# A ConvNeXt block in two phases: every third block stored whole, 96-row reloads, and all loads of phase 2 on the SyncE queue

## The chip, the core and the metric

The kernel runs on one core of a Trainium2 chip. That core has five engines with a queue of instructions each: TensorE (PE, matrix products; its weight loads are listed as PEld), VectorE (DVE), ScalarE (ACT), GpSimd (POOL) and SyncE (SP, which here only issues transfers). Data moves between the chip's memory (HBM) and the on-chip buffers through 16 DMA engines. A transfer can be issued from the queue of SP (the profile's q1, "hardware_dynamic") or from that of GpSimd (q0, "software_dynamic"); both use the same 16 engines. The metric is the device time of one execution, in microseconds (us). The kernel before takes 1479.7 us, the median of three runs from 1476.99 to 1480.79.

## The reference, cut to what matters

```python
# x: (1, 512, 512, 96) bf16; dw: (3, 3, 96); w1: (96, 384); w2: (384, 96)
out = depthwise_conv3x3(x, dw)                     # zero padding
h = layernorm(out, axis=-1)                        # over the 96 channels, no scale
h = gelu(einsum('bhwc,ce->bhwe', h, w1))
gx = sqrt((h * h).sum(axis=(1, 2)) + 1e-6)         # over the whole image, per channel
nx = gx / (gx.mean(axis=-1) + 1e-6)
h = grn_gamma * (h * nx) + grn_beta + h
return x + einsum('bhwe,ec->bhwc', h, w2)
```

The sum `gx` runs over the whole image. So nothing can be multiplied with `w2` before every pixel has gone through the gelu once, and the hidden tensor `h` (512 x 512 x 384 in bf16, some 201 MB) is far too big to be kept on chip.

## The kernel before, in words

The image is cut into 128 blocks of four rows (2048 pixels). `yn` is a block after the convolution and the layernorm, 96 channels by 2048 pixels; `g` is the same block after `w1` and gelu, 128 x 6144 values (1536 KB).

**Phase 1** (to about 980 us) makes `yn` and `g` of every block and gathers the sums of squares. Its order is written out by hand: one block enters per slot, and in a slot stand the convolution, the normalisation, the matrix product with `w1`, the gelu and the squares of different blocks. `yn` of every block is written to HBM (`stage_write`) and read back as a 96-row tile `ynT` (`stage_read`, from SP), since the product wants channels on the partitions. The squares are made in two ways: a block's `g` has four quarters, and `cm_quads(q)` says how many of them VectorE handles (`BATCH_NORM_STATS2`); the others go to TensorE (`gram_next`). Blocks for which `is_whole(q)` holds have their `g` written to HBM, in three pieces of 512 KB, one in each following slot (`store_next`); there are 35 of these, `q % 10` being 0, 3 or 7 below block 114. Five blocks (`HELD`) keep `g` on chip, three (`KEPT`) keep `ynT`. Phase 1 ends with the sums and the scaled weights `W2s`.

**Phase 2** (from about 980 us) goes through the 128 blocks in the order `ORDER`, which spreads the 40 blocks that have their `g` among the 88 that must make it again. A position n needs:

- its `g`: kept on chip, or loaded from `g_dram` into one of two buffers `gl` (1536 KB; called G here), or made again from `ynT` (Y here). Y has a ring of six buffers, and making `g` again takes four units of three matmuls of 512 columns and one gelu of 128 x 1536 each (`cm_unit`), run about two blocks ahead of use (`LEAD`, `pace`), with three buffers `gr`.
- its `x`: loaded into one of five buffers `xr` (384 KB; X here). GpSimd adds the bias to it and writes `xb` (`stage_xb`), two positions ahead.
- the product: `stage_mm2` runs four parts of 12 matmuls with `W2s`; after each part VectorE adds `xb` and writes a quarter of `o_sb` (four buffers).
- the store of `o_sb` to the output (384 KB; O here), issued from SP one position later (`stage_out`).

G and X for position n + 5 (`PRE`) are issued in position n. In phase 2 of the kernel before, SP issues Y and O, GpSimd issues G and X between its additions. The first eight positions (`FIRST`) keep the written order; behind them the scheduler of the language orders each queue, and it puts a Y some ten positions ahead of its use, where it waits for its buffer in the ring.

`yn_rows(q)` reads Y as 128 rows of 4 KB, the 96 rows of block q and 32 of the next one. The weights `w1p` have zeros in rows 96 to 127, so the extra rows add nothing. `yn_src(q)` reads the 96 rows alone; phase 1 uses it.

In the profile most instructions carry line 35, that of the helper `InOrder` which records them, so groups are told apart by their tiles. Lines of their own are 279 (X), 290 (G), 294 (Y), 324 (`xb`) and 352 (O).

Of the kernel before, what the change touches and what calls it, by code (L numbers as in the profile page):

```python
# [12 lines left out]
GR = 4  # L13
# [3 lines left out]
FILL = (6, 15)  # L17
BATCH = 4
NHELD = 5
WHOLE = (0, 3, 7)  # L20
NTAIL = 14
GRB = 3

# [33 lines left out]
def kernel(  # L57
# [16 lines left out]
    B, H, W, C = x.shape  # L74
# [6 lines left out]
    NBLK = H // GR  # L81
# [5 lines left out]
    yn_dram = dram.tile([NBLK, C, GR * W], bf16, name="yn_dram")  # L87
    r_dram = dram.tile([NBLK, GR, W], bf16, name="r_dram")

    TAIL0 = NBLK - NTAIL  # L90
# [3 lines left out]
    def is_held(q):  # L94
        return q in HELD

    def is_whole(q):
        return q < TAIL0 and q % 10 in WHOLE

    def cm_quads(q):  # L100
        if is_whole(q) or is_held(q):
            return NQ
        if q > HELD[0]:
            return 1
        return 2 if q >= NBLK - 16 or (q - 1) % 10 in WHOLE else 3

    whole = [q for q in range(NBLK) if is_whole(q)]
    g_dram = dram.tile([len(whole), 128, NQ * NCH * QW], bf16, name="g_dram")

# [11 lines left out]

    def yn_src(q):
        return yn_dram[q].rearrange("c (r w) -> c r w", r=GR)

    def yn_rows(q):
        return yn_dram[q:q + 2].rearrange("q c (r w) -> (q c) r w", r=GR)[0:128]

    def yn_dst(q, r):
        return yn_dram[q].rearrange("(c i) (r w) -> r c i w", i=NI, r=GR)[r]
# [17 lines left out]
    B2bc_f = consts.tile([128, C], f32, name="B2bc_f")  # L147

    NENT = sum(cm_quads(q) for q in range(NBLK - 2))
    NLAST = cm_quads(NBLK - 2) + cm_quads(NBLK - 1)  # L150
    GROUPS = [min(32, NENT - k) for k in range(0, NENT, 32)] + [NLAST]
    NACC = len(GROUPS)
# [9 lines left out]
    W2s = consts.tile([128, NCH, C], bf16, name="W2s")  # L162
    B2c = consts.tile([128, C], f32, name="B2c")
    free = [[q for q in range(NBLK) if is_whole(q)], list(HELD)]
    free = [v for i, q in enumerate(free[0]) for v in (free[1][i:i + 1] + [q])]
    made_q = KEPT + [q for q in range(NBLK) if not is_whole(q) and not is_held(q) and q not in KEPT]
# [17 lines left out]
    with ExitStack() as p1:  # L184
# [57 lines left out]
        for b in range(min(2, NBLK)):  # L242
# [3 lines left out]
                       in_=zrow[:, None, :NI * GR * 32].to_broadcast([128, 3, NI * GR * 32]), func=ACTF.Identity)  # L246
# [28 lines left out]
        def load_xr(n, pq):  # L275
            q = ORDER[n]
            r0 = q * GR
            xr = late.xr.tile([128, PXP, C], bf16, name="xr")
            pq.dma_start(out=xr[:], in_=x[0, r0:r0 + GR].rearrange("r w c -> (r w) c").rearrange(  # L279
                "(p g) c -> p g c", g=PXP))  # L280
            grp.setdefault(q, {})["xr"] = xr

        def load_rest(n, sq, pq):
            q = ORDER[n]
            v = grp.setdefault(q, {})
            if is_held(q):
                v["g"] = gs[q]
            elif is_whole(q):
                v["g"] = late.gl.tile([128, NQ, NCH, QW], bf16, name="gl")
                pq.dma_start(out=v["g"][:].rearrange("p t j w -> p (t j w)"), in_=g_dram[whole.index(q)])  # L290
            else:
                ynt = yn_ring[SLOTS[nth_made[q] % NYT]]
                if q not in KEPT:
                    sq.dma_start(out=ynt[:], in_=yn_rows(q))
                v["ynt"] = ynt

        def recompute(q, t):
# [22 lines left out]
        def stage_xb(q, pq, bias):  # L320
            if q is None:
                return
            xb = late.xb.tile([128, PXP, C], f32, name="xb")
            pq.tensor_tensor(out=xb[:], in0=grp[q]["xr"][:],  # L324
                                    in1=bias[:, None, :].to_broadcast([128, PXP, C]), op=ALU.add)
            grp[q]["xb"] = xb

        def stage_mm2(n, q):
            g, xb = grp[q]["g"], grp[q]["xb"]
            GQ = QW // 128  # L330
            o_sb = late.o.tile([128, PXP, C], bf16, name="o_sb")
            for sub in range(NSUB):
                O = out_bank()
                for gl_ in range(GPS):
                    gg = sub * GPS + gl_
                    for j in range(NCH):
                        t, c = gg // GQ, gg % GQ * 128
                        pe.matmul(O[:, gl_, :], lhsT=g[:, t, j, c:c + 128], rhs=W2s[:, j, :],
                                   start=(j == 0), stop=(j == NCH - 1))
                dve.tensor_tensor(out=o_sb[:, sub * GPS:(sub + 1) * GPS, :], in0=O,  # L340
                                   in1=xb[:, sub * GPS:(sub + 1) * GPS, :], op=ALU.add)
                if n == NBLK - 1:
                    out_part(q, o_sb, sub)
                if sub == NSUB - 1 and q in nth_made:
                    used[0] += 1
                pace(n, sub)
            grp.pop(q)
            return o_sb

        def stage_out(q, o_sb):  # L350
            r0 = q * GR
            nc.sync.dma_start(
                out=out[0, r0:r0 + GR].rearrange("r w c -> (r w) c").rearrange("(p g) c -> p g c", g=PXP),
                in_=o_sb[:])

        PRE = 5
# [42 lines left out]
        n = 0  # L399
# [255 lines left out]
        for q in range(NBLK):  # L655
            if q == NBLK - 2:
                e_ = 32 * (NACC - 1)
            ents[q] = e_
            e_ += cm_quads(q)
# [166 lines left out]
        for s in range(last_slot + 1):  # L826
# [120 lines left out]
            if s == last_slot:  # L947
                for n in range(PRE):
                    load_rest(n, sp, sp)
# [19 lines left out]
        r = gi[:].bitcast(f32)  # L969
        for it in range(3):  # L970
# [5 lines left out]
            r = rn_[:]  # L976
# [21 lines left out]
    with p2:  # L998
        def out_part(q, o_sb, sub):
            r0 = q * GR  # L1000
            nc.sync.dma_start(
                out=out[0, r0:r0 + GR].rearrange("r w c -> (r w) c").rearrange(
                    "(p g) c -> p g c", g=PXP)[:, sub * GPS:(sub + 1) * GPS],
                in_=o_sb[:, sub * GPS:(sub + 1) * GPS])

        held = None
        FIRST = 8
        for n, q in enumerate(ORDER):
            sq, pq = (sp, pool) if n < FIRST else (nc.sync, nc.gpsimd)
            if n + PRE < NBLK:  # L1010
                load_rest(n + PRE, sq, pq)
                load_xr(n + PRE, pq)
            if 3 <= n + 2 < NBLK:
                stage_xb(ORDER[n + 2], pq, B2c)
            if n == NBLK - 1:
                stage_out(*held)
                held = None
            o_sb = stage_mm2(n, q)
            if held:
                stage_out(*held)  # L1020
            held = (q, o_sb)
# [30 lines left out]
```

## Time and profile before

| What | us or share |
|---|---|
| times of the three runs | 1480.79, 1479.70, 1476.99 |
| profiled execution: span from first to last instruction | 1480.8 |
| PE, ACT, POOL, DVE busy, share of the span | 94%, 96%, 88%, 80% |
| POOL and ACT busy in phase 2, 1100 to 1450 us | 338.1 and 335.7 of 350 |
| DMA engines busy, 300 to 850 us and 1100 to 1450 us | 0.83 and 1.02 |
| bytes moved per second in the same stretches | 261 and 410 GB/s |
| granted TensorE clock, mean | 0.994 |

The profiled execution's span equals the longest of the three times within rounding. A busy share says how long an engine had an instruction in hand in a stretch. "Idle before" of a group of instructions is how long its engine waited in front of them, and the name behind the arrow is what ended the wait. The DMA share is the mean over the 16 engines of the time that packets took; packets that overlap on an engine can bring it a little above 1. The three resources TensorE, ScalarE and GpSimd are all busy for 96 to 97% of the stretch from 1100 to 1450 us, and the DMA engines for all of it.

### The profile page before, as it was taken

Reading aid. Unit: us, or ns where it says so; the run is one execution under the profiler, and the core shown is the slowest. Engines: PE = TensorE matmul, PEld = TensorE weight load, DVE = VectorE, ACT = ScalarE, POOL = GpSimd, SP = SyncE. Lnnn points to the kernel's source line nnn. Section 1 sums busy time; section 2 is a strip of 40 time slices with the busy share of each in tenths; the row PEclk is TensorE's granted clock in tenths of the full one; section 3 lists DMA queues with packets and bytes.
Section 4 is the critical chain, followed back from the end, with each engine's and each line's share of the span. In section 5 each row is a group of like instructions: output and inputs, shape, how many; then the busy total and the mean of one; then the engine's idle time right before and its main releaser. Section 6 shows DMA issues by size and latency. Waiting matters only on the chain.

```text
span 1480.8 us, 54225 instructions
## 1 busy us (share of the span) xinstructions
PE 1391.3 (94%) x23125; PEld 810.4 (55%) x23125; DVE 1182.0 (80%) x2135; ACT 1414.4 (96%) x1595; POOL 1300.3 (88%) x922
## 2 busy tenths in 40 slices
PE   8888999999999999999999997789999999999998
PEld 3434444444444444444444445467777777776776
DVE  7849989999999999999999987965555555555555
ACT  7888989999999999999999999999999999999997
POOL 3459889998998999998999987569999999999997
PEclk9999999999999999999999999999999999999999
DMA  5568788788888888888888866669999999999997
GB/s 180 179 205 255 241 253 280 228 271 260 260 248 264 258 264 255 276 253 254 263 258 266 263 216 195 195 225 409 366 359 402 417 416 413 419 410 417 411 412 282
DMA packets 167768, 433.08 MB, mean 292 GB/s; under 512 B 31558, under 2 KB 81318, under 8 KB 163046
## 3 DMA queue, kind: packets, MB, share of 16 engines
q1 hardware_dynamic: 151284, 326.04, 66.3%
q0 software_dynamic: 14880, 103.43, 17.6%
q8 instruction: 181, 2.97, 0.8%
q14 instruction: 61, 0.50, 0.1%
q10 hardware_dynamic: 1362, 0.15, 0.1%
HBM read 273.30 MB, written 156.22 MB: 290 GB/s over the span
## 4 chain that ended last, share of the span: by engine, by line
PE 30%; ACT 24%; DMA 19%; POOL 13%; DVE 6%; issue 4%; SPq 4%; POOLq 0%; ACTq 0%; DVEq 0%
PE PS L35 30%; ACT g L35 16%; DMA out_dram<-o_sb 9%; POOL yn L35 6%; ACT y_bf L35 5%; POOL ysq L35 5%; SPq L35 4%; DMA yn_dram<-yn 3%; DVE bst L35 3%; DMA xin<-in_x_dram 2%; DMA rbc<-r_dram 2%; DMA ynT<-yn_dram 1%; DMA g_dram<-g 1%; DVE o_sb L35 1%; ACT xT L35 1%
## 5 line engine op out<-in xcount | busy, mean ns | idle before, releaser
L35 ACT ACTIVATE g<-PS 128x512 bf16<-128x512 f32 (+2 forms) x1062 | 727.7, 864 | 16.5 <-PE PS L35 15.6
L35 DVE BATCH_NORM_STATS2 bst<-g 128x6 f32<-128x512 bf16 x1110 | 671.3, 672 | 35.4 <-ACT g L35 34.5
L35 PE MATMUL PS<-ynT,w1p 128*128 128x512 bf16 x2181 | 609.6, 381 | 23.6 <-ACT g L35 5.4
L35 ACT ACTIVATE gr<-PS 128x1536 bf16<-128x1536 f32 x360 | 498.5, 1459 | 18.8 <-PE PS L35 13.8
L35 POOL TENSOR_TENSOR yn<-y_bf,rbc 128x1536 bf16<-128x1536 bf16 x126 | 391.3, 3108 | 77.3 <-ACT rbc L35 21.9
L35 DVE TENSOR_TENSOR o_sb<-PS,xb 128x384 bf16<-128x384 f32 x512 | 277.3, 556 | 227.0 <-PE PS L35 190.1
L324 POOL TENSOR_TENSOR xb<-xr,B2c 128x1536 f32<-128x1536 bf16 x118 | 368.1, 3133 | 4.3 <-DVE o_sb L35 2.0
L35 PE MATMUL PS<-xT,Wq 64*32 64x511 bf16 (+1 forms) x9198 | 340.5, 389 | 26.2 <-ACT y_bf L35 8.1
L35 POOL TENSOR_TENSOR ysq<-y_bf 128x1536 bf16<-128x1536 bf16 x114 | 313.6, 2752 | 12.8 <-ACT y_bf L35 12.8
L35 PEld LDWEIGHTS <-w1p 128*128 128x128 bf16 x2181 | 171.6, 98 | 222.0 <-issue 133.4
L35 PEld LDWEIGHTS <-gr 128*128 128x128 bf16 x4296 | 212.1, 98 | 68.9 <-issue 12.0
L35 PE MATMUL PS<-W2s,gr 128*128 128x96 bf16 x4224 | 223.5, 206 | 8.2 <-DVE o_sb L35 8.0
L35 PEld LDWEIGHTS <-Wq 64*32 64x32 bf16 x9216 | 111.9, 90 | 193.3 <-issue 145.9
L35 ACT ACTIVATE y_bf<-PS 128x1536 bf16<-128x1536 f32 (+2 forms) x135 | 199.4, 1482 | 17.4 <-PE PS L35 13.3
L35 DVE STREAM_TRANSPOSE xT<-xin 128x576 f32<-128x576 f32 (+1 forms) x256 | 181.4, 748 | 8.1 <-DMA xin<-in_x_dram 8.1
L35 PEld LDWEIGHTS <-g 128*128 128x128 bf16 x1704 | 104.9, 98 | 86.3 <-issue 54.3
L35 PE MATMUL PS<-w1p,ynT 128*128 128x256 bf16 (+2 forms) x822 | 125.8, 273 | 8.0 <-ACT xT L35 3.2
L35 PE MATMUL PS<-g 128*128 128x128 bf16 x1464 | 122.6, 220 | 2.9 <-DVE PS L35 2.6
L35 PEld LDWEIGHTS <-gl 128*128 128x128 bf16 x1680 | 82.8, 98 | 26.8 <-issue 5.0
L35 PE MATMUL PS<-W2s,gl 128*128 128x96 bf16 x1680 | 89.5, 206 | 3.4 <-DVE o_sb L35 3.2
L35 PEld LDWEIGHTS <-ynT 128*128 128x128 bf16 x822 | 64.1, 97 | 31.5 <-issue 13.7
L279 POOL DMA_DIRECT2D xr<-in_x_dram x115 | 63.7, 555 | 14.2 <-POOL xb L324 14.2
(105 smaller groups left out, 576.5 us busy)
## 6 DMA issues: line engine op xcount, KB each, us to landing
xin<-in_x_dram SPq DMA_DIRECT2D x126, 432.0 KB
g_dram<-g SPq DMA_DIRECT2D x105, 512.0 KB
gl<-g_dram POOLq DMA_DIRECT2D x35, 1536.0 KB, 11.3
yn_dram<-yn SPq DMA_DIRECT2D x512, 96.0 KB
ynT<-yn_dram SPq DMA_DIRECT2D x128, 384.0 KB
out_dram<-o_sb SPq DMA_DIRECT2D x127, 384.0 KB
xr<-in_x_dram POOLq DMA_DIRECT2D x123, 384.0 KB, 6.9
ynT<-yn_dram SPq DMA_DIRECT2D x85, 512.0 KB
```

The source lines that it names most:

```text
L35: r = f(*a, **k)
L279: pq.dma_start(out=xr[:], in_=x[0, r0:r0 + GR].rearrange("r w c -> (r w) c").rearrange("(p g) c -> p g c", g=PXP))
L324: pq.tensor_tensor(out=xb[:], in0=grp[q]["xr"][:], in1=bias[:, None, :].to_broadcast([128, PXP, C]), op=ALU.add)
```

## The change

Three things change together. Every third block below 114 is stored whole: 38 blocks, so that 85 are made again instead of 88, and `cm_quads` follows the new pattern. Phase 2 reads Y as the 96 rows of its block (384 KB instead of 512 KB). G and X of phase 2 are issued from SP, like Y and O; GpSimd issues no transfer there.

```diff
-WHOLE = (0, 3, 7)
...
     def is_whole(q):
-        return q < TAIL0 and q % 10 in WHOLE
+        return q < TAIL0 and q % 3 == 0
...
-        return 2 if q >= NBLK - 16 or (q - 1) % 10 in WHOLE else 3
+        return 2 if q >= NBLK - 16 or q % 3 == 1 else 3
...
-    def yn_rows(q):
-        return yn_dram[q:q + 2].rearrange("q c (r w) -> (q c) r w", r=GR)[0:128]
...
-                    sq.dma_start(out=ynt[:], in_=yn_rows(q))
+                    sq.dma_start(out=ynt[:C], in_=yn_src(q))
...
             if n + PRE < NBLK:
-                load_rest(n + PRE, sq, pq)
-                load_xr(n + PRE, pq)
+                load_rest(n + PRE, sq, sq)
+                load_xr(n + PRE, sq)
```

In the built program of the changed kernel, SP's queue in phase 2 holds, position after position, the load for n + 5 (Y or G, where there is one), X for n + 5, and O for n - 1.

## The prediction

> **What bounds the kernel now.** I read the page's slices first, to see the stages, then the busy table by stage.
>
> ```profile
> DMA  5568788788888888888888866669999999999997
> GB/s 180 179 205 255 241 253 280 228 271 260 260 248 264 258 264 255 276 253 254 263 258 266 263 216 195 195 225 409 366 359 402 417 416 413 419 410 417 411 412 282
> ```
> ```profile
> core 0: us, PE busy (x) PEld busy (x) DVE busy (x) ACT busy (x) POOL busy (x), PEclk, DMA share, GB/s
> 300.00:850.00 550.00, 527.12 (x9544) 259.14 (x9543) 544.63 (x933) 546.12 (x777) 515.84 (x384) 1.00 0.83 261
> ...
> 980.00:1100.00 120.00, 118.46 (x1739) 88.12 (x1738) 66.96 (x124) 117.25 (x86) 113.99 (x67) 1.00 0.98 370
> 1100.00:1450.00 350.00, 340.60 (x4962) 251.78 (x4959) 190.88 (x353) 335.74 (x243) 338.14 (x205) 1.00 1.02 410
> ```
>
> Phase 1 is held by ACT and DVE (99% busy), and DMA has room (0.83). Phase 2 runs at a flat 410 GB/s with every DMA engine busy. VectorE makes four `o_sb` quarters per block, so 353 in 350 us are 88.25 blocks: 3.966 us a block. Next, the groups and the waits of that stretch:
>
> ```profile
> L35 ACT ACTIVATE gr<-PS 128x1536 bf16<-128x1536 f32 x243 | 336.5, 1451 | 14.3 <-PE PS L35 10.7 <-ACT gr L35 0.3
> ...
> L324 POOL TENSOR_TENSOR xb<-xr,B2c 128x1536 f32<-128x1536 bf16 x89 | 277.6, 3134 | 1.6 <-DVE o_sb L35 0.6
> ...
> L279 POOL DMA_DIRECT2D xr<-in_x_dram x88 | 48.8, 555 | 10.1 <-POOL xb L324 10.1
> ```
> ```profile
> DVE o_sb L35 <- DMA out_dram<-o_sb: 30.8, 21, 2.7
> ```
>
> The 30.8 us say who is slowest: VectorE finds all four `o_sb` still on their way out, and TensorE then waits 9.3 us for VectorE. The chain of waits has stores of 12.6 to 14.0 us from issue to landing at just these places. So DMA sets the pace, with the engines close behind. Per block ACT needs 336.5/243 = 1.385 us for each of 2.75 units, 3.81 us. GpSimd needs 3.13 + 0.555 + 0.32 x 0.536 = 3.86 us. TensorE: in the timeline 12 matmuls of `stage_mm2` alone take 0.51 us (1213.09 to 1213.60), with one unit behind them 1.15 us (1213.60 to 1214.75), so a unit is 0.64 and a block 4 x 0.51 + 2.75 x 0.64 = 3.80 us.
>
> **The change, part by part.** Last, the transfers of 1100 to 1450 us (queues: packets, MB, share of the 16 engines' time; issues: count, size, median us from issue to landing):
>
> ```profile
> q0 software_dynamic: 10952, 77.23, 54.1%
> q1 hardware_dynamic: 21194, 65.66, 46.9%
> ...
> gl<-g_dram POOLq DMA_DIRECT2D x28, 1536.0 KB, 11.4
> out_dram<-o_sb SPq DMA_DIRECT2D x89, 384.0 KB
> xr<-in_x_dram POOLq DMA_DIRECT2D x88, 384.0 KB, 7.0
> ynT<-yn_dram SPq DMA_DIRECT2D x59, 512.0 KB
> ```
>
> *Bytes.* Before, 16 positions hold 5 G, 11 Y, 16 X, 16 O: 5 x 1536 + 11 x 512 + 32 x 384 = 25600 KB, 1600 KB a block. After, 3 positions hold 1 G, 2 Y, 3 X, 3 O: 1536 + 2 x 384 + 6 x 384 = 4608 KB, 1536 KB a block. That is 4.0% less: more G, cheaper Y. At the same rate a block takes 3.966 x 0.96 = 3.81 us.
>
> *Is a 96-row Y really 25% cheaper?* Its price lies between 384 and 512 parts of the old one. The nearest row is a 96-row read of phase 1 that was almost alone, from 28.1 to 28.5 us:
>
> ```profile
> DMA packets 37, 0.14 MB, mean 348 GB/s; under 512 B 3, under 2 KB 3, under 8 KB 37
> ...
> q1 hardware_dynamic: 37, 0.14, 84.9%
> ```
>
> 348/0.849 = 410 GB/s per full share, the rate of phase 2 with 128 rows (410/1.02 = 402). So I price it by bytes. The other end, 512 as before, gives 1536 + 1024 + 2304 = 4864 KB, 1621 KB a block, 4.02 us.
>
> [...]
>
> *One queue.* X and G move from q0 to q1. By the rows above q0 moves 77.23 MB in 0.541 x 350 us of 16 engines, 25.5 GB/s each, and q1 25.0. So the moved 54% may cost 2% more: 1.1% of 3.81, 0.04 us; the other end is nothing, since G keeps its long rows. I take 0.03: 3.84 us. Whether a single queue holds the rate is read where q0 was nearly empty, 1112.3 to 1113.7 us:
>
> ```profile
> q1 hardware_dynamic: 187, 0.60, 105.9%
> q0 software_dynamic: 1, 0.00, 0.0%
> ```
>
> It does: 430 GB/s over that stretch, stores and reads mixed. The far end is phase 1, where SP's queue alone made 261/0.83 = 314 GB/s, with many packets under 2 KB: 1573 kB/314 = 5.0 us.
>
> *SP's own time.* An issue takes 0.33 us there (0.43 for an X; a G by the nearest row, a 512 KB store of phase 1, 0.37 to 0.72): three a block, at most 1.5 of 3.84 us. G waits for TensorE to leave the block one before the current one (two `gl` buffers, six positions apart); X and O stand behind it, but O waits for VectorE's end of the same block anyway, some 0.6 us later. Cost nothing; without that cover, at the list's last G (positions 125 and 127 lie close), one O comes a block late. Y is issued 5 positions ahead instead of ten; it is wanted about 2.3 positions ahead, and SP reaches it almost a block early, so 3.3 x 3.84 = 12.7 us are left against the landings of 7 to 14 us. That is tight, like the store's own slack of three blocks; late loads are the dangerous rival.
>
> *Engines.* GpSimd loses its issues: 3.13 us a block. ACT makes 2.67 units: 3.69 us. TensorE: 3.75 us by the sum above; from 1040 to 1100 us, at 364 GB/s, it did 16 blocks in 60 us, 3.75 each, with 2.75 units. So once the stores stop holding VectorE, TensorE is next, 0.1 us below the DMA. This caps the gain.
>
> *Phase 1.* Nine more store pieces of 512 KB. One piece goes per slot and three fall due per three slots, so none queue up; DMA share goes from 0.83 to about 0.86. VectorE's quarters stay 370 against 369. Bounds: 0, and 9 x 1.27 us (512 KB at 410 GB/s) = 11 us if each were exposed; ACT at 99% covers them, I take 1 us. The same for the end of the list: 1 us.
>
> *Sum.* From 1100 us on there are 353 + 32 quarters, 96 blocks: 96 x (3.966 - 3.84) = 12.1 us. From 980 to 1100, 31 blocks at 3.87, mostly held by TensorE: 2 us. Less the 2 us of phase 1 and the end: 12 us. 1480.8 - 12 = 1468.8 in the profiled execution; the median of the runs lies 1.1 us lower, so 1468.
>
> **The rivals.**
>
> *The 96 rows cost as much as 128.* For: only the short isolated read speaks against it. Then 96 x 0.054 = 5 us lost in the steady part, nothing won before it, 2 lost: 1487. Chance 0.17.
>
> *One queue in order makes loads late* (the other side: slower). Place: Y behind O on SP, and every transfer behind a G of 1.57 MB, 3.8 us at 410 GB/s. For: store landings are already 14 us at saturation, and Y's lead is halved. Against: what comes late lowers the demand, and a full queue keeps the rate; a stall costs only when the engines run dry. It decides from 0.126 us a block, 0.4 us in three blocks; one microsecond per three blocks is 96/3 - 12 = 20 us over, 1501; at phase 1's rate of 314 GB/s it would be 96 x 1.04 = 100 us over. Chance 0.15.
>
> *The gain is half.* TensorE, ACT and DMA lie within 4% and disturb each other, or phase 1 pays for the nine pieces: 3.90 us a block or 6 us in phase 1, 1474. Chance 0.14.
>
> That the change does not do what it says I exclude: the built queues hold 38 G, 82 Y of 96 rows, and no transfer on GpSimd in phase 2.
>
> **How the numbers follow.** The main case has 0.54. A measurement of this kernel can tell about 0.3%, 4.4 us, from no change. The main case and half of the "half" case lie beyond that: faster 0.54 + 0.07 = 0.61. The other half of it and the lower edge of the first rival: same 0.07 + 0.02 = 0.09. The rest of the first rival and the second: slower 0.15 + 0.15 = 0.30. The main case alone spans 1462 (pace 3.78, near TensorE's floor) to 1473. The range goes from 1460 to 1494, which takes in the first rival and the beginning of the second.
>
> **What would show it.** In the middle of phase 2: 3.84 us a block (about 91 blocks in 350 us), still some 405 to 410 GB/s at a DMA share near 1, all in q1; waits of `o_sb` for stores below 30.8 us; GpSimd near 82% busy; gelu of `gr` at 2.67 a block; phase 2 beginning near 980 us. Wrong if TensorE or ACT wait for `ynT` or `gl` (late loads), if the rate per DMA share falls with 96-row reads in flight (first rival), or if phase 2 begins later than 983 us.

## The result and the profile after

The changed kernel takes 1540.05 us (median of four runs), the kernel before 1478.35 us beside it: a ratio of 1.0402, 95% interval 1.0363 to 1.0441. It is 4% slower where 0.8% faster was forecast, and it lies outside the range. One of the four executions of e1_rows96 below took 1904 us at a granted clock of 0.654 and is left out of its ratio.

The page's slices of the changed kernel, DMA busy share and bytes moved, show that phase 1 is as before and phase 2 is not:

```profile
DMA  5668788887888888888888756699999999999997
GB/s 174 196 201 251 248 268 269 269 280 252 267 266 255 262 283 269 278 269 277 264 268 260 238 158 204 232 353 351 357 343 341 350 324 341 341 347 330 338 336 275
```

Phase 2 starts at the same time (the first `o_sb` is written at 973.1 us, before at 975.5) and lasts longer (to 1535.4, before 1477.4). The busy table of 1100 to 1450 us:

```profile
core 0: us, PE busy (x) PEld busy (x) DVE busy (x) ACT busy (x) POOL busy (x), PEclk, DMA share, GB/s
...
1100.00:1450.00 350.00, 297.82 (x4209) 219.75 (x4207) 161.84 (x301) 280.53 (x201) 233.87 (x76) 0.97 1.02 340
```

VectorE wrote 301 quarters instead of 353, so a block takes 350/75.25 = 4.65 us, before 3.97. All engines are less busy than before; only the DMA share is unchanged at 1.02, and with it the engines moved 340 GB/s instead of 410. The transfers of that stretch:

```profile
q1 hardware_dynamic: 30939, 118.44, 101.1%
...
gl<-g_dram SPq DMA_DIRECT2D x25, 1536.0 KB
xr<-in_x_dram SPq DMA_DIRECT2D x75, 384.0 KB
out_dram<-o_sb SPq DMA_DIRECT2D x74, 384.0 KB
ynT<-yn_dram SPq DMA_DIRECT2D x50, 384.0 KB
```

118.44 MB in 1.011 x 350 us of 16 engines is 20.9 GB/s each; before, the two queues made 25.0 and 25.5. The bytes per block did fall to 1573 kB, and 1573 kB at 340 GB/s are 4.63 us: the whole loss is the rate. The waits of the same stretch have the face of late loads and stores (line numbers are one to four lower in the changed kernel: the helper's is 34, X 275, G 286, Y 290, `xb` 320, O 348):

```profile
DVE o_sb L34 <- DMA out_dram<-o_sb: 84.4, 35, 4.9
POOL xb L320 <- DMA xr<-in_x_dram: 75.8, 28, 4.9
ACT gr L34 <- PE PS L34: 66.7, 45, 5.2
```

But late transfers alone don't show a bad order of issues here, where the 16 DMA engines have no idle time (share 1.02). A lower rate looks the same from the engines, and e3 below, with the same order and queue, decides between the two. The chain of waits from 1200 to 1300 us passes from transfer to transfer, nearly without an engine in it:

```profile
1189.66 12.52 DMA xr<-in_x_dram
...
1202.19 12.76 DMA ynT<-yn_dram
...
1215.01 13.16 DMA out_dram<-o_sb
```

### The profile page after: what moved, and what is told of

It reads as the page before. It is cut to its first block, busy times and chain, and to the rows that moved or that the text cites. A ratio compares the mean times of both kernels' runs of the same rounds, so it can differ in the third digit from the quotient of the medians.

```text
span 1538.6 us, 54241 instructions
## 1 busy us (share of the span) xinstructions
PE 1395.2 (91%) x23104; PEld 815.9 (53%) x23104; DVE 1180.2 (77%) x2132; ACT 1402.6 (91%) x1583; POOL 1215.5 (79%) x764
## 4 chain that ended last, share of the span: by engine, by line
DMA 37%; ACT 24%; PE 15%; POOL 11%; SPq 5%; issue 4%; DVE 3%; POOLq 0%; ACTq 0%; DVEq 0%
ACT g L34 17%; PE PS L34 15%; DMA out_dram<-o_sb 12%; DMA ynT<-yn_dram 9%; DMA xr<-in_x_dram 6%; POOL yn L34 6%; ACT y_bf L34 5%; SPq L34 5%; POOL ysq L34 4%; DMA yn_dram<-yn 3%; DMA gl<-g_dram 2%; DMA rbc<-r_dram 2%; DMA xin<-in_x_dram 2%; DVE bst L34 1%; ACT xT L34 1%
## 5 line engine op out<-in xcount | busy, mean ns | idle before, releaser
L34 ACT ACTIVATE gr<-PS 128x1536 bf16<-128x1536 f32 x348 | 486.6, 1455 | 89.0 <-PE PS L34 84.0
L34 PEld LDWEIGHTS <-w1p 128*128 128x128 bf16 x2142 | 168.5, 98 | 222.1 <-issue 125.9
L34 PEld LDWEIGHTS <-gl 128*128 128x128 bf16 x1824 | 89.2, 98 | 26.7 <-issue 3.7
L34 PE MATMUL PS<-W2s,gl 128*128 128x96 bf16 x1824 | 95.8, 206 | 2.7 <-DVE o_sb L34 2.6
L34 PE MATMUL PS<-rowsel,ysq 128*128 128x4 bf16 x1536 | 56.6, 166 | 11.9 <-POOL ysq L34 11.2
```

The lines of the kernel that those rows point to most:

```text
L34: r = f(*a, **k)
```

## The experiments

Three edits came together, so most runs take one, two or the whole of them. Two theories stood against each other: the **rows theory** (a load of 96 rows slows the packets on the DMA engines, its own and its neighbours') and the **queue theory** (a single queue, served in order, loses the rate or makes loads late). Every ratio below is to the kernel before on the same chip, with its 95% interval; us a block is 350 us over a quarter of the `o_sb` writes from 1100 to 1450 us. e7, e8 and e11 were executed twice each, the others four to twelve times. Three kernels serve for their times alone: e4 leaves out one of a block's four image rows, e8 32 of its 96 channels, and e7 puts every second Y beside the wrong weights.

| Run | Y | G, X from | whole | ratio | us a block | GB/s |
|---|---|---|---|---|---|---|
| before | 128 rows | GpSimd | 35 | 1 | 3.97 | 410 |
| after | 96 | SP | 38 | 1.0402 (1.0363 to 1.0441) | 4.65 | 340 |
| e1_rows96 | 96 | GpSimd | 35 | 1.0139 (1.0105 to 1.0173) | 4.22 | 369 |
| e2_spq | 128 | SP | 35 | 0.9974 (0.9944 to 1.0005) | 3.95 | 411 |
| e3_after_128rows | 128 | SP | 38 | 1.0035 (1.0007 to 1.0063) | 4.02 | 411 |
| e4_after_128x3k | 128 x 3 KB | SP | 38 | 0.9934 (0.9909 to 0.9960) | 3.85 | 405 |
| e5_after_gpsimd | 96 | GpSimd | 38 | 1.0188 (1.0128 to 1.0247) | 4.23 | 374 |
| e6_whole38 | 128 | GpSimd | 38 | 1.0018 (0.9988 to 1.0048) | 4.03 | 412 |
| e7_after_alternate | 96, in turn low and high | SP | 38 | 1.0373 (1.0292 to 1.0454) | 4.50 | 353 |
| e8_after_64rows | 64 | SP | 38 | 1.0272 (1.0175 to 1.0368) | 4.39 | 337 |
| e9_spq_rows96 | 96 | SP | 35 | 1.0386 (1.0339 to 1.0433) | 4.53 | 339 |
| e10_after_y_gpsimd | 96, from GpSimd | SP | 38 | 1.0266 (1.0225 to 1.0308) | 4.38 | 357 |
| e11_after_112rows | 112 | SP | 38 | 1.0557 (1.0498 to 1.0616) | 4.79 | 339 |
| e12_spq_33whole | 128 | SP | 33 | 1.0015 (0.9990 to 1.0040) | 3.98 | 400 |

### One edit alone

The 96 rows alone, on the kernel before:

```diff
-                    sq.dma_start(out=ynt[:], in_=yn_rows(q))
+                    sq.dma_start(out=ynt[:C], in_=yn_src(q))
```

> The kernel before with one edit: phase 2 reads Y as 96 rows; 35 whole blocks, G and X still from GpSimd. Rows theory (a 96-row load slows the DMA engines' packets, its own and those beside it): most of the 60 us of the whole change is here, 1515 to 1545 us, with 340 to 370 GB/s at a DMA share near 1 in the middle of phase 2 and packets' time per byte up. Queue theory (it is the single queue in order that loses the rate): 96 rows save 1408 of 25600 KB per 16 blocks, DMA falls behind the engines, 3.80 us a block instead of 3.97, 1462 to 1470 us.

It is 1.39% slower, about 21 us, though a block of phase 2 moves 5.5% fewer bytes. The queue theory, which wanted a gain here, falls; the rows theory has the sign right but had expected most of the 60 us. The transfers of e1 from 1100 to 1450 us:

```profile
q0 software_dynamic: 10439, 73.87, 57.5%
q1 hardware_dynamic: 18163, 54.54, 42.5%
```

q0 holds G and X, which this edit doesn't touch. It made 77.23 MB at 54.1% before (25.5 GB/s on each engine) and 73.87 MB at 57.5% here: 22.9. So a 96-row load makes the loads beside it dearer, not only itself.

The queue alone, on the kernel before:

```diff
-                load_rest(n + PRE, sq, pq)
-                load_xr(n + PRE, pq)
+                load_rest(n + PRE, sq, sq)
+                load_xr(n + PRE, sq)
```

> The kernel before with one edit: all loads of phase 2 from SP; 35 whole blocks, Y of 128 rows. Rows theory: within 10 us of the kernel before (1470 to 1490), DMA still near 405 GB/s. Queue theory: 1515 to 1545 us, rate near 340 GB/s, waits for ynT, gl and xr on PE, DVE and POOL.

No difference that can be told: 0.9974, the interval just reaches 1. The busy row of 1100 to 1450 us and its one queue:

```profile
1100.00:1450.00 350.00, 342.66 (x4996) 253.66 (x4994) 192.29 (x354) 338.04 (x246) 277.86 (x89) 1.00 1.02 411
```
```profile
q1 hardware_dynamic: 37589, 143.24, 101.5%
```

One queue moves 411 GB/s, what two moved; GpSimd falls from 338.1 to 277.9 us busy, and nothing follows, since it was not the one in front. The queue's own waits of this run hold a warning for readers:

```profile
SPq L352 <- DMA gl<-g_dram: 79.7, 24, 4.1
SPq L279 <- DMA out_dram<-o_sb: 45.5, 76, 1.3
```

A store on SP here ends its wait when a G lands, which it doesn't need. In this program a transfer on SP uses the completion semaphore of the transfer eight before it on the queue, so at most eight are under way: 226 of the 264 issues of this stretch begin within 0.15 us of that landing, and none before it. In the changed kernel the same two waits stand first and third in SP's list, with 114.5 and 39.7 us. They look like the culprit there, and in e2 they cost nothing.

The whole blocks alone, on the kernel before:

```diff
-        return q < TAIL0 and q % 10 in WHOLE
+        return q < TAIL0 and q % 3 == 0
...
-        return 2 if q >= NBLK - 16 or (q - 1) % 10 in WHOLE else 3
+        return 2 if q >= NBLK - 16 or q % 3 == 1 else 3
```

> The kernel before with one edit: 38 whole blocks instead of 35. Y of 128 rows, G and X from GpSimd. 1621 KB a block instead of 1600: 96 blocks x 0.05 us = 5 us slower, 1483 to 1492 us, at 410 GB/s. If the three extra blocks weighed more in phase 1 (nine more store pieces), phase 2 begins more than 3 us later than before.

1.0018, within the interval no difference in the total; in the middle of phase 2 a block takes 4.03 us, as the 1621 KB say (4.02). The first `o_sb` came at 978.6 us, 3.1 later than before; but among these runs it lies between 971.2 and 985.8 in no order by the number of whole blocks, so nothing is read from it.

### Is it the bytes or the rows?

The changed kernel, Y read as 128 rows again (this run and the next define `yn_rows` as in the kernel before):

```diff
...
-                    sq.dma_start(out=ynt[:C], in_=yn_src(q))
+                    sq.dma_start(out=ynt[:], in_=yn_rows(q))
```

> The changed kernel with Y read as 128 rows again (38 whole blocks, all loads from SP). 1621 KB a block instead of 1600. Rows theory: 4.02 us a block, 1480 to 1492 us, no stretched packets. Queue theory: as slow as the changed kernel or slower, 1535 to 1560 us.

1.0035: with more bytes, the 4% are gone. Then the same 384 KB as the changed kernel, in 128 rows of 3 KB:

```diff
...
-                    sq.dma_start(out=ynt[:C], in_=yn_src(q))
+                    sq.dma_start(out=ynt[:, 0:3], in_=yn_rows(q)[:, 0:3])
```

> The changed kernel with Y read as 128 rows of 3 KB, the same 384 KB as its 96 rows of 4 KB (the last image row of each block is left out of the load, so the made-again blocks are computed with old data there; the work is the same). Same bytes, same queue, other layout. Rows theory: the pace that the bytes allow, 3.81 to 3.85 us a block, 1465 to 1475 us. Queue theory, and any theory of bytes: no better than the changed kernel, 1530 to 1545 us.

It is faster than the kernel before by 0.66%, at 3.85 us a block; the 1476.0 us are 1 us over the range of the rows theory. VectorE's busy time with its number of instructions (the `o_sb` quarters), the clock, the DMA share and GB/s from 1100 to 1450 us, first of the changed kernel, then of e3, then of e4:

```profile
1100.00:1450.00 350.00, 161.84 (x301) 0.97 1.02 340
```
```profile
1100.00:1450.00 350.00, 187.33 (x348) 1.00 1.02 411
```
```profile
1100.00:1450.00 350.00, 196.17 (x364) 1.00 1.02 405
```

All three have the same queue, the same order and the same share of DMA time. e4 has the bytes of the changed kernel, in rows of 3 KB that lie apart in HBM. e3 has more bytes, in rows of 4 KB without gaps, like those of the changed kernel. Both keep the rate, so neither the bytes nor the length of a row is the reason. What is left, and shown as the cause, is the number of rows, which is the number of partitions that a load writes. By the two ratios 69 us lie between the changed kernel and e4 (0.0468 of 1480).

The single packets in the traces agree (1100 to 1450 us; in these runs only Y has packets of 4 KB there, X and O have 3 KB). In e3 the median packet of 3 KB takes 121 ns, and 0.4% take over one and a half times as long. In the changed kernel the median is 125 ns, but 20% are over that mark, and a tenth take 221 ns or more. A 3 KB packet that begins there with no Y packet under way takes 131 ns in the mean, with three to nine Y packets under way 172 ns; in e3 it is 122 ns either way. So the loss comes while a 96-row load is in flight, and falls heavily on some packets rather than evenly on all.

### What about the rows?

Partitions 0 to 95 are three quarters of 128, so the lower half of the buffer takes twice the bytes of the upper. If that were it, putting every second load on partitions 32 to 127 would even it out:

```diff
-                    sq.dma_start(out=ynt[:C], in_=yn_src(q))
+                    p0 = 32 * (nth_made[q] % 2)
+                    sq.dma_start(out=ynt[p0:p0 + C], in_=yn_src(q))
```

> The changed kernel with the 96 rows of every second Y put on partitions 32 to 127 instead of 0 to 95 (the made-again blocks then have channels on the wrong weights; the work is the same). Each half of the partitions now gets the same bytes over two loads. If the slow-down is that the lower 64 partitions carry more bytes than the upper ones, it goes: 3.85 to 3.95 us a block, 1470 to 1485 us. If it is that a 96-row load spreads its rows over the engines in another way than a 128-row one, so that engines meet at the same partitions, it stays: 1525 to 1545 us.

It stays slow: 1.0373, not to be told from the changed kernel. In the one profile of each, a block in the middle takes 4.50 instead of 4.65 us, not the 3.85 to 3.95 of the first theory. The halves are even here over two loads, not within one.

Two other numbers of rows, first 64:

```diff
-                    sq.dma_start(out=ynt[:C], in_=yn_src(q))
+                    sq.dma_start(out=ynt[:64], in_=yn_src(q)[:64])
```

> The changed kernel with only the first 64 rows of each Y loaded (channels 64 to 95 are left out and hold old data; the work of the engines is the same). 256 KB instead of 384 KB, 1451 KB a block. If bytes count, DMA needs 3.60 us a block and TensorE sets 3.75: 1455 to 1465 us. [...]

And 112, the 96 of the block and 16 of the next one:

```diff
+    def yn_rows(q):
+        return yn_dram[q:q + 2].rearrange("q c (r w) -> (q c) r w", r=GR)[0:112]
...
-                    sq.dma_start(out=ynt[:C], in_=yn_src(q))
+                    sq.dma_start(out=ynt[:112], in_=yn_rows(q))
```

> The changed kernel with Y read as 112 rows, 448 KB (38 whole blocks, all loads from SP): 16 rows more than the change, 16 fewer than 128. By bytes it lies between the 128-row form (1490 us) and what the bytes of 96 would give: 1480 to 1488 us. If every number of rows but 128 meets the other loads at the same partitions, 1515 to 1550 us.

64 rows, half the bytes of 128, are 2.7% slower than before (1524.1 us, 1455 to 1465 if bytes counted); 112 rows are the slowest of all, 5.6%, and beyond the 1550 us that either theory allowed (1565.6). The queue of e8 and of e11 from 1100 to 1450 us:

```profile
q1 hardware_dynamic: 30650, 117.25, 101.5%
```
```profile
q1 hardware_dynamic: 30635, 118.20, 101.8%
```

That is 20.6 and 20.7 GB/s on each engine, with the changed kernel's 20.9 the same rate to 2%. So it is not a matter of how many bytes: on one queue each of the three numbers of rows other than 128 lowers the rate of everything to 337 to 340 GB/s, 0.82 to 0.83 of the 411 that 128 rows keep, and at that rate the bytes give the pace (64 rows: 1486 kB a block at 337 GB/s, 4.41 us, measured 4.39; 112 rows: 1617 kB at 339, 4.77, measured 4.79). Why the number of rows does this is not shown. That engines meet at the same partitions, the second theory of e7 and of e11, is the author's supposition: no trace here shows which engine writes where. What is measured is that a tenth of the changed kernel's 3 KB packets take 221 ns or more and half of them 125 or less.

### Why 21 us alone and 57 with SP's queue?

> The kernel before with two of the three edits: Y of 96 rows and all loads from SP; 35 whole blocks. If the two edits only add, 96 rows 21 us and SP -4 us: 1495 to 1505 us. If a single queue makes a 96-row load dearer than two queues do, as the sum of the whole change says (60 us against 28 with GpSimd's queue): 1515 to 1535 us, 340 to 355 GB/s.

The edit is that of e1 and that of e2 together. 1.0386, slower than either theory gave: 96 rows and one queue make the whole loss without the 38 blocks. Its row, VectorE's part as above:

```profile
1100.00:1450.00 350.00, 167.14 (x309) 0.97 1.01 339
```

On the changed kernel, G and X back on GpSimd's queue:

```diff
-                load_rest(n + PRE, sq, sq)
-                load_xr(n + PRE, sq)
+                load_rest(n + PRE, sq, pq)
+                load_xr(n + PRE, pq)
```

> The changed kernel with G and X issued from GpSimd again (38 whole blocks, Y of 96 rows). If the 96 rows cost the same whichever queue the other loads use, 1530 to 1545 us as the changed kernel. If a second queue softens it (the 96 rows alone, with G and X from GpSimd, cost 21 us), 1500 to 1515 us, 365 to 375 GB/s.

1.0188 instead of 1.0402. And two queues split the other way, only Y on GpSimd's:

```diff
-                load_rest(n + PRE, sq, sq)
+                load_rest(n + PRE, pq, sq)
```

> The changed kernel with only Y moved to GpSimd's queue (38 whole blocks, Y of 96 rows; G, X and O from SP). Two queues again, but split the other way. If it is the interleaving of two queues on each DMA engine that softens a 96-row load, 1500 to 1520 us. If only G and X on GpSimd's queue do (larger packets, or fewer transfers on SP), 1530 to 1550 us as the changed kernel.

1.0266, or 1522 us: 2 us beyond what the interleaving theory gave and 8 below what the other gave. The rate of the two queues there:

```profile
q1 hardware_dynamic: 26586, 103.28, 81.3%
q0 software_dynamic: 5936, 20.86, 18.7%
```

q1, without Y, made 22.7 GB/s on each engine, q0, with nothing but Y, 19.9. So a second queue softens the loss whichever transfers it holds, and doesn't remove it. Why it does is not shown: the interleaving of e10's theory is the author's supposition, and no trace here shows the order of packets on an engine. A rival is as open: SP's limit of eight transfers. In the changed kernel 217 of SP's 224 issues begin within 0.15 us of the landing of the eighth before, in e1 and e5, with two queues, none. The limit alone costs nothing (251 of 258 issues in e3, at 411 GB/s), and in e10, where 18 of 187 meet it, a good part of the loss is still there; but no run changes it under 96 rows.

### A version to beat both

```diff
-WHOLE = (0, 3, 7)
+WHOLE = (0, 3)
...
-        return q < TAIL0 and q % 10 in WHOLE
+        return q < TAIL0 and q % 7 in WHOLE
...
-        return 2 if q >= NBLK - 16 or (q - 1) % 10 in WHOLE else 3
+        return 2 if q >= NBLK - 16 or (q - 1) % 7 in WHOLE else 3
```

This is made on e2.

> A version to beat both: Y of 128 rows, all loads from SP, and 33 whole blocks (block number mod 7 being 0 or 3), 90 made again. DMA per block falls to some 1582 KB, 3.92 us at 410 GB/s, ACT rises to 3.89 us, GpSimd stays at 3.13: 1470 to 1478 us if the three can run that close together; 1480 to 1490 if ACT becomes the bound.

1.0015: no gain. From 1100 to 1450 us ACT is busy for 340.3 and TensorE for 343.1 us, the DMA share stays at 1.02 and the rate falls to 400 GB/s; a block takes 3.98 us, more than the 3.92 forecast for the bytes and the 3.89 for ACT. Which of the three holds it is not shown: in that stretch VectorE waits 139.1 us for TensorE and 19.7 us for stores, ScalarE 7.5 us for TensorE, and GpSimd 15.5 us for `xr`. No run that computes the whole result beats the kernel before by more than its interval.

## Why the prediction was wrong

- **DMA bounds phase 2, and bytes over rate give the pace:** right for loads of 128 rows. 1621 KB gave 4.02 and 4.03 us a block (forecast 4.02), and e4, which has the bytes that were forecast with 128 rows, 3.85 (forecast 3.84) and 10 us won (forecast 12).
- **"So I price it by bytes":** the step that failed. It counted 384 KB for a 96-row Y and left the rate of the DMA engines at 410 GB/s; the runs show the rate falling, to 369 GB/s on two queues and 339 to 340 on one. The read of 28.1 to 28.5 us had hardly any neighbours, and a load in a full queue has many. It was also the quick part of that read, which took about 2 us and not one (its packets begin from 27.0 to 29.0 us). Just before, still alone, the same read made 184/0.641 = 287 GB/s per full share, for a reason that no run shows:

```profile
DMA packets 27, 0.11 MB, mean 184 GB/s; under 512 B 0, under 2 KB 0, under 8 KB 27
...
q1 hardware_dynamic: 27, 0.11, 64.1%
```

The nearest row under load stood in phase 1, where 96-row reads run among other transfers at a share of 0.83. From 300 to 850 us a packet of 4 KB (a read of Y or a store of `g`) takes 198 ns in the mean, in phase 2 with 128 rows (reads of Y alone) 162 ns; the prediction put phase 1's lower rate down to small packets, which take a quarter of the packets' time there. No run shows how much of that is due to the 96 rows. The far end of the price was wrong too: it took 512 KB as the most that a 96-row load could cost, which leaves out that it slows the others. e1 shows 25.5 to 22.9 GB/s on G and X, and the changed kernel 4.65 us a block where that end gave 4.02.

- **The first rival** was the right place, and its sign came: the rate at a DMA share of 1.02 fell from 410 to 340 GB/s with 96-row reads in flight. But its price was 5 us; measured are 21 us on two queues and about 57 on one. The price of a 128-row load gave 4.02 us a block, too little against 4.65, and in e7 an even load on the halves over two loads didn't bring the time back (4.50 us).
- **One queue holds the rate:** right for 128 rows (411 GB/s, no gain and no loss; the 0.03 us taken for it was nothing). What the step missed is that one queue makes the price of the 96 rows more than twice as high (about 57 us in e9, 21 in e1), so the three were not to be summed.
- **The second rival, late loads:** its signs appeared (75.8 us of waits for `xr`), its cause did not: the DMA share stayed at 1.02, and e3 with the same queue, order and leads has the rate back (411 GB/s).
- **SP's own time, GpSimd's relief, phase 1 and the nine store pieces:** nothing measurable, as taken or nearly (1 us). The limit of eight transfers on SP isn't in the prediction, and e2 and e3 show that it costs nothing with 128 rows (411 GB/s in both). GpSimd in e4, at the forecast pace, is busy for 284.4 of 350 us, 81%, forecast 82%.
- **The range** ended at 1494 because for the rows it took a price, not a rate, as what could change. A lower rate had a price only as the far end of the single queue, in the second rival (phase 1's 314 GB/s, 100 us over), and the range took in no more than its beginning.

## What to carry to other kernels

In this stage, bound by transfers, the edit that saved bytes by changing the number of partitions had two prices: the bytes (5.5% fewer a block in e1 and e9), and the rate of everything that shares the DMA engines (410 to 369 GB/s with two queues, 411 to 339 with one). Look for the shape in the trace under a full load before pricing it; here 128 rows with a quarter of ballast were cheaper than the 96 that were wanted (1.0035 against 1.0402). And test combined edits singly: one of these, the single queue, cost nothing alone (0.9974) and made another nearly three times as dear (about 57 us instead of 21).

## What was not expected of the hardware

- A load's number of rows lowered the rate of its neighbours: G and X went from 25.5 to 22.9 GB/s on each engine when only Y changed from 128 to 96 rows.
- 112 rows are worse than 96, and 64 rows (256 KB) are slower than 128 (512 KB): ratios 1.0557, 1.0402, 1.0272 against 1.0035.
- The granted TensorE clock was a little lower in the runs in which TensorE was less busy: from 1100 to 1450 us 0.97 with 297.8 us busy in the changed kernel, 0.96 with 292.7 at 112 rows and 0.98 with 326.2 in e1, against 1.00 with 340.6 before.
